# Another emission order for the same steps of a fused RWKV-6 and SwiGLU kernel, with casts, copies and masks dealt anew over the engines

## The chip, the cores and the metric

The kernel runs on one core of a Trainium2 chip. The core has five engines with a list of instructions each: TensorE (PE in the profile) for matrix products and transposes, VectorE (DVE), ScalarE (ACT), GpSimd (POOL) and SyncE (SP), which here only issues transfers. Each engine works through its own list in order and waits where an operand isn't there yet. The metric is the device time of one execution in microseconds; less is better.

## The reference

A linear-attention layer with a decaying state (RWKV-6) feeds an RMS norm and a gated feed-forward block. Cut to what is computed:

```python
batch, n_heads, seq, head_dim = (4, 8, 768, 48)
for t in range(S):
    cur = np.einsum('bhd,bhe->bhde', u[None] * kt, vt)
    y[:, :, t] = np.einsum('bhd,bhde->bhe', rt, state + cur)
    state = wt[:, :, :, None] * state + np.einsum('bhd,bhe->bhde', kt, vt)
...
n_tokens, d_model, d_ff = (3072, 384, 1536)
xn = x / np.sqrt(np.mean(x * x, axis=-1, keepdims=True) + 1e-06) * rms_g
g = xn @ w_gate
return (g * (1.0 / (1.0 + np.exp(-g))) * (xn @ w_val)) @ w_out
```

Inputs and output are float32.

## The kernel before

The sequence is cut into six blocks n of 128 positions, and there are four batches j, so there are 24 chunks (n, j) of 128 rows and 384 columns. For each chunk the kernel does the attention as matrix products over the 128 positions, then the norm; for each group of four chunks (512 rows) it does the feed-forward block.

The steps are small functions with arguments (n, j), or (n, f) in the feed-forward block, and their names are the words of the list:

- Loads on SP's queue: `load_r`, `load_k`, `load_v`, `load_w` (L256 to L280), 192 KB each; the four `load_w.0.j` bring 384 KB, two blocks at once. They go into rings of 8 buffers (4 for w). The weights of the feed-forward block come through POOL's queue: `load_gv`, `load_wo` (L348, L353).
- Decay: `ln` (ACT), `cs_mm` (PE, sums of logarithms), `cs_add` (DVE), `exp_r` and `exp_k` (ACT), `w_tot` (DVE), then `r_mul` (DVE) and `k_mul` (DVE or POOL, L457) scale r and k.
- Transposes of the scaled r and k: in blocks 0 and 1 `rk_pe` on PE and a copy `rk_tr` on DVE or ACT (L484); from block 2 on `rk_tr` is a transposing DMA from SP's queue.
- Scores and output: `q_mm` (PE; from block 2 on one step does two chunks), the mask `q_mask_e` (DVE) for the even heads, and for the odd heads either a masked copy on DVE or a plain copy on ACT (`q_copy_o`) and a mask on POOL (`q_mask_o`, L510 to L518); `cast_v` (ACT or POOL, L384); `y_mm` (PE). The bonus term is `bonus_mul` (POOL, two instructions), `bonus_sum` (DVE), `bonus_v` (POOL). The state is `st_mm` (PE) and `st_new` (DVE).
- Norm: `x_add` (DVE), `x_sq` (ACT), `x_rstd` (two instructions on ACT, or two on POOL, L560), `xn_mul` (ACT). The normed chunk is transposed into the operand of the feed-forward block by `xn_pe` and `xn_out` (PE, DVE), in blocks 4 and 5 by a transposing DMA `xn_tr` and `xn_gain` (POOL).
- Feed-forward block of group n: twelve `gate_mm` (PE, three matmuls of 512 columns), `silu` (ACT), twelve `val_mm` (PE), `h_mul` (DVE); then for each 128 rows `o_mm` (PE, twelve matmuls of 384 columns), `o_out` (DVE or ACT, L663) and `out_dma` (SP). Group 0 is made of the chunks 0.0, 0.1, 1.0, 1.1, and group 1 of 0.2, 0.3, 1.2, 1.3. The last 128 rows are done in two halves, `o_mm.5.3` and `o_mm.5.4`.

What sets the order is the list `ORDER` (L25 to L126): the kernel calls the steps in this order and every engine's list, SP's too, is that order with the other engines' steps left out. A suffix such as `:4` puts so many filler matmuls on a matrix of zeros in front of the step; they keep PE busy and compute nothing that is used. Accumulator banks come from three small rings (`psum`, L228): two banks each for gate and value products, four for everything else; the next step that needs a bank gets the one whose last reader stands earliest in the list, and PE waits for that reader. Eight sets of chunks (L175 to L189) say which engine does the steps that can be done by two: `CAST_ACT` (the cast of v on ACT rather than POOL), `K_POOL` (the k product on POOL rather than DVE), `RK_DVE` (the copy of the transposed chunk on DVE rather than ACT), `ODD_DVE` (the odd heads' mask on DVE rather than ACT and POOL), `RSTD_ACT` (the inverse root on ACT rather than POOL) and `OUT_DVE` (the output copy on DVE rather than ACT). ACT holds one table of functions at a time, one for Ln and Exp and one for Silu; `act` (L247) loads the other one (L249) when the list changes between them.

Of the kernel before, what the change touches and what calls it, by code (L numbers as in the profile page):

```python
# [41 lines left out]
gate_mm.0.2 gate_mm.0.0 rk_pe.0.2 silu.0.0 silu.0.2 val_mm.0.2 q_mask_e.0.3 h_mul.0.0 gate_mm.0.5 gate_mm.0.1 silu.0.5  # L42
silu.0.1 val_mm.0.1 rk_tr.0.2 q_copy_o.0.3 h_mul.0.1 bonus_mul.0.3 bonus_sum.0.3 h_mul.0.2 gate_mm.0.6:1
gate_mm.0.11:1 q_mm.0.2 cast_v.0.2 silu.0.6 silu.0.11 q_mask_o.0.2 gate_mm.0.8 val_mm.0.6 q_mask_e.0.2 cast_v.0.3
st_mm.0.2 val_mm.0.11 q_mask_o.0.3 h_mul.0.6 val_mm.0.5 y_mm.0.3 y_mm.0.2 bonus_sum.0.2 bonus_v.0.2 load_wo.0.0
load_wo.1.0 bonus_v.0.3 silu.0.8 h_mul.0.11 cs_mm.1.2 load_wo.2.0 h_mul.0.5 exp_k.1.2 x_add.0.2 st_new.0.2 exp_r.1.2
k_mul.1.2 cs_mm.1.3 exp_k.1.3 st_mm.0.3 exp_r.1.3 val_mm.0.8 val_mm.0.7 w_tot.1.2 r_mul.1.2 x_add.0.3 gate_mm.0.4
w_tot.1.3 r_mul.1.3 rk_pe.1.2 gate_mm.0.7 k_mul.1.3 h_mul.0.8 silu.0.4 x_sq.0.3 bonus_mul.1.2 x_rstd.0.3 rk_tr.1.2
silu.0.7 rk_pe.1.3 gate_mm.0.10 val_mm.0.4 h_mul.0.7 x_sq.0.2 rk_tr.1.3 load_k.2.1 load_k.2.3 load_v.2.1 load_v.2.0
load_k.2.2 q_mm.1.2 val_mm.0.9 cast_v.1.2 xn_mul.0.3 silu.0.10 q_copy_o.1.2 h_mul.0.4 q_mask_o.1.2 gate_mm.0.9  # L50
xn_pe.0.3 val_mm.0.10 st_new.0.3 q_mm.1.3 bonus_sum.1.2 x_rstd.0.2 q_mask_e.1.2 xn_out.0.3 y_mm.1.2 h_mul.0.10
q_mask_e.1.3 silu.0.9 h_mul.0.9 o_mm.0.3 ln.2.1 xn_mul.0.2 bonus_v.1.2 bonus_mul.1.3 q_mask_o.1.3 st_mm.1.2 xn_pe.0.2
cs_mm.2.1 ln.2.0 x_add.1.2 cs_add.2.1 x_sq.1.2 cs_mm.2.0 exp_r.2.1 o_out.0.3 xn_out.0.2 x_rstd.1.2 cast_v.1.3
cs_add.2.0 bonus_sum.1.3 w_tot.2.1 ln.2.3 exp_k.2.1 exp_r.2.0 o_mm.0.0 y_mm.1.3 xn_mul.1.2 o_out.0.0 bonus_v.1.3
r_mul.2.0 x_add.1.3 exp_k.2.0 ln.2.2 x_sq.1.3 o_mm.0.2 o_out.0.2 w_tot.2.0 r_mul.2.1 x_rstd.1.3 st_mm.1.3 cs_mm.2.3
xn_pe.1.2 cs_add.2.3 xn_out.1.2 cs_mm.2.2 exp_r.2.3 cs_add.2.2 load_k.3.3 w_tot.2.3 o_mm.0.1 xn_mul.1.3 r_mul.2.3
st_new.1.2 exp_k.2.2 val_mm.1.1 gate_mm.1.1 exp_r.2.2 exp_k.2.3 w_tot.2.2 val_mm.1.2 xn_pe.1.3 r_mul.2.2 gate_mm.1.2
st_new.1.3 silu.1.1 silu.1.2 k_mul.2.0 bonus_mul.2.0 out_dma.0.0 k_mul.2.1 cast_v.2.1 k_mul.2.3 h_mul.1.1 rk_tr.2.0
rk_tr.2.1 gate_mm.1.3 silu.1.3 bonus_mul.2.2 k_mul.2.2 xn_out.1.3 bonus_sum.2.0 h_mul.1.2 val_mm.1.5 gate_mm.1.4
silu.1.4 val_mm.1.4 rk_tr.2.3 gate_mm.1.8 st_mm.2.1 gate_mm.1.5 silu.1.8 h_mul.1.4 val_mm.1.8 load_v.2.2 silu.1.5  # L60
cast_v.2.0 st_new.2.1 rk_tr.2.2 o_out.0.1 h_mul.1.8 gate_mm.1.9 gate_mm.1.10 val_mm.1.3 load_w.3.3 load_v.2.3
load_r.3.3 load_w.3.1 out_dma.0.3 load_w.3.0 out_dma.0.1 load_r.3.0 bonus_v.2.0 bonus_mul.2.3 bonus_sum.2.2 h_mul.1.5
bonus_mul.2.1 cast_v.2.2 load_k.3.0 load_w.3.2 q_mm.2.0 load_k.3.1 silu.1.9 silu.1.10 q_copy_o.2.1 h_mul.1.3
q_mask_o.2.0 q_mask_e.2.0 q_mask_e.2.1 gate_mm.1.7 gate_mm.1.0 silu.1.0 val_mm.1.0 y_mm.2.0 gate_mm.1.6 val_mm.1.9
bonus_sum.2.3 h_mul.1.0 x_add.2.0 load_r.3.1 x_sq.2.0 silu.1.6 out_dma.0.2 h_mul.1.9 val_mm.1.10 h_mul.1.10 q_mm.2.2
gate_mm.1.11 val_mm.1.6 cast_v.2.3 q_copy_o.2.2 silu.1.7 silu.1.11 ln.3.0 x_rstd.2.0 xn_mul.2.0 q_mask_e.2.3
bonus_sum.2.1 q_mask_e.2.2 q_mask_o.2.1 load_v.3.3 load_w.4.1 load_r.3.2 ln.3.1 bonus_v.2.1 bonus_v.2.2 q_mask_o.2.3
h_mul.1.6 q_mask_o.2.2 bonus_v.2.3 st_mm.2.0 st_new.2.0 o_mm.1.0 y_mm.2.1 load_k.3.2 x_add.2.1 y_mm.2.3 val_mm.1.7
y_mm.2.2 cs_mm.3.0 st_mm.2.3 val_mm.1.11 x_add.2.3 x_sq.2.3 ln.3.3 x_sq.2.1 xn_pe.2.0 cs_mm.3.1 o_out.1.0 o_mm.1.1
out_dma.1.0 h_mul.1.7 cs_add.3.0 exp_k.3.0 x_add.2.2 cs_add.3.1 st_new.2.3 x_rstd.2.3 xn_mul.2.3 ln.3.2 x_sq.2.2  # L70
# [643 lines left out]
```

## Time and profile before

| what | value |
|---|---|
| time, median of 3 runs (lowest, highest) | 203.93 us (203.73, 204.25) |
| profiled execution: span from the first to the last instruction | 202.2 us; its time isn't listed apart |
| mean granted TensorE clock in it | 0.998 |
| DVE busy | 157.5 us, 307 instructions |
| ACT busy | 135.0 us, 278 instructions |
| POOL busy | 124.4 us, 178 instructions |
| moved by DMA | 32.42 MB, 160 GB/s over the span |

A row of the profile that groups instructions reads: line of the kernel, engine, operation, what is written from what is read by tile names, count, total busy time, mean nanoseconds of one, and then the idle time of the engine just before them with what ended it. A row of the timeline begins with start and duration in microseconds; in square brackets stand the idle time before it and its releaser. Rows of PEld are weight loads, which run beside the matmuls of PE. A row of the waits names who waited, for whom, the total, how often, and the longest. Matmuls are pipelined and their recorded ends reach past the start of the next one, so PE is read here by distances between starts.

### The profile page before, as it was taken

Reading aid. Unit: us, or ns where it says so; the run is one execution under the profiler, and the core shown is the slowest. Engines: PE = TensorE matmul, PEld = TensorE weight load, DVE = VectorE, ACT = ScalarE, POOL = GpSimd, SP = SyncE. Lnnn points to the kernel's source line nnn. Section 1 sums busy time; section 2 is a strip of 40 time slices with the busy share of each in tenths; the row PEclk is TensorE's granted clock in tenths of the full one; section 3 lists DMA queues with packets and bytes.
Section 4 is the critical chain, followed back from the end, with each engine's and each line's share of the span. In section 5 each row is a group of like instructions: output and inputs, shape, how many; then the busy total and the mean of one; then the engine's idle time right before and its main releaser. Section 6 shows DMA issues by size and latency. Waiting matters only on the chain.

```text
span 202.2 us, 4604 instructions
## 1 busy us (share of the span) xinstructions
PE 191.3 (95%) x1677; PEld 121.9 (60%) x1694; DVE 157.5 (78%) x307; ACT 135.0 (67%) x278; POOL 124.4 (62%) x178
## 2 busy tenths in 40 slices
...
GB/s 144 231 234 207 212 208 202 195 179 208 206 184 225 160 212 191 210 185 188 199 176 215 237 188 203 183 190 108 134 179 104 0 23 99 0 117 0 63 115 99
DMA packets 121567, 32.42 MB, mean 160 GB/s; under 512 B 116420, under 2 KB 120392, under 8 KB 121544
## 3 DMA queue, kind: packets, MB, share of 16 engines
...
q8 instruction: 13, 0.21, 0.4%
q14 instruction: 10, 0.08, 0.1%
...
HBM read 25.96 MB, written 4.72 MB: 152 GB/s over the span
## 4 chain that ended last, share of the span: by engine, by line
PE 65%; ACT 3%; DMA 2%; DVE 2%; issue 1%; SPq 0%; DVEq 0%; ACTq 0%
PE ps_av L617 7%; PE ps_bu L617 7%; PE ps_au L617 7%; PE ps_bv L617 6%; PE ps_qx L660 6%; PE ps_qv L660 6%; PE ps_qu L660 5%; PE ps_qz L660 4%; PE ps_au L622 2%; PE ps_bu L622 2%; DMA rkT<-rk 2%; PE ps_av L622 2%; PE ps_bv L622 2%; ACT L249 1%; PE ps_au L419 1%; PE ps_qv L500 1%
## 5 line engine op out<-in xcount | busy, mean ns | idle before, releaser
L660 PEld LDWEIGHTS <-ht 128*128 128x128 bf16 x300 | 28.1, 98 | 17.5 <-DVE ht L646 1.0
L251 ACT ACTIVATE sg<-ps_av 128x512 bf16<-128x512 f32 x36 | 21.5, 597 | 22.8 <-PE ps_av L617 18.0
L646 DVE TENSOR_TENSOR ht<-ps_bv,sg 128x512 bf16<-128x512 f32 x29 | 19.9, 687 | 13.9 <-PE ps_bv L617 12.9
L251 ACT ACTIVATE sg<-ps_au 128x512 bf16<-128x512 f32 x36 | 21.5, 596 | 11.5 <-PE ps_au L617 7.7
L617 PEld LDWEIGHTS <-wg_sb 128*128 128x128 bf16 x180 | 19.2, 114 | 15.9 <-issue 0.6
L617 PEld LDWEIGHTS <-wv_sb 128*128 128x128 bf16 x180 | 19.2, 114 | 15.7 <-issue 0.5
L465 POOL TENSOR_TENSOR ruk<-rt,kt 128x384 f32<-128x384 f32 x24 | 24.0, 1001 | 3.7 <-DMA kt<-in_k_dram 2.8
L475 POOL TENSOR_TENSOR ydiag<-vt,diag 128x384 f32<-128x384 f32 x24 | 20.4, 859 | 9.4 <-DVE diag L470 9.1
L617 PE MATMUL ps_av<-xnt,wg_sb 128*128 128x512 bf16 x88 | 25.0, 381 | 0.3
L466 POOL TENSOR_TENSOR ruk<-ruk,u_bc 128x384 f32<-128x384 f32 x24 | 24.0, 1001 | 1.9
L617 PE MATMUL ps_bu<-xnt,wv_sb 128*128 128x512 bf16 x86 | 24.8, 380 | 0.4
L646 DVE TENSOR_TENSOR ht<-ps_bu,sg 128x512 bf16<-128x512 f32 x31 | 21.3, 686 | 4.8 <-PE ps_bu L617 3.1
L617 PE MATMUL ps_au<-xnt,wg_sb 128*128 128x512 bf16 x87 | 23.6, 380 | 0.1
L617 PE MATMUL ps_bv<-xnt,wv_sb 128*128 128x512 bf16 x82 | 23.2, 380 | 0.2
L459 POOL TENSOR_TENSOR rk<-kt,ek 128x384 bf16<-128x384 f32 x16 | 15.9, 1001 | 9.7 <-ACT ek L251 5.9
L249 ACT ACT_TABLE_LOAD x14 | 18.0, 1283 | 1.9 <-PEq L698 1.6
L660 PE MATMUL ps_qx<-wo_sb,ht 128*128 128x384 bf16 x96 | 17.1, 326 | 0.2 <-DVE ht L646 0.2
L558 ACT ACTIVATE junk<-xb 128x384 bf16<-128x384 f32 x24 | 12.5, 522 | 6.3 <-DVE xb L553 6.2
L571 ACT ACTIVATE xn<-xb,rstd 128x384 bf16<-128x384 f32 x24 | 14.2, 609 | 0.6 <-POOL rstd L567 0.5
L470 DVE TENSOR_REDUCE diag<-ruk 128x8 f32<-128x384 f32 x24 | 13.1, 544 | 1.9 <-POOL ruk L466 1.9
L660 PE MATMUL ps_qv<-wo_sb,ht 128*128 128x384 bf16 (+1 forms) x84 | 13.8, 314 | 0.0
L251 ACT ACTIVATE lw<-wt 128x384 bf16<-128x384 f32 (+1 forms) x20 | 11.6, 583 | 2.8 <-DMA wt<-in_w_dram 2.7
...
## 6 DMA issues: line engine op xcount, KB each, us to landing
...
```

The lines of the kernel that those rows point to most:

```text
L249: nc.scalar.preload_act_table_set(table_name)
L251: return nc.scalar.activation(**kw).ins
L459: eng.tensor_tensor(out=rk[:, n % 2, j, 1, :, 0:D], in0=inp["k", n, j], in1=bank["cs_k", n, j][:, 0:DM].rearrange("p (h d) -> p h d", h=H) ...
L465: nc.gpsimd.tensor_tensor(out=ruk[n, j], in0=inp["r", n, j], in1=inp["k", n, j], op=ALU.mult)
L466: nc.gpsimd.tensor_tensor(out=ruk[n, j], in0=ruk[n, j], in1=u_bc, op=ALU.mult)
L470: nc.vector.tensor_reduce(out=diag[n, j].rearrange("p h o -> p (h o)"), in_=ruk[n, j], axis=mybir.AxisListType.X, op=ALU.add)
L475: nc.gpsimd.tensor_tensor(out=ydiag[n, j], in0=inp["v", n, j], in1=diag[n, j].to_broadcast([128, H, D]), op=ALU.mult)
L571: nc.scalar.activation(out=xn, in_=xb[n, j], func=AF.Copy, scale=rstd[n, j][:, 1:2])
L617: nc.tensor.matmul(ps, lhsT=units(ws, c, f), rhs=x[:, c, :], start=(c == 0), stop=(c == KC - 1))
L622: nc.tensor.matmul(ps[:, i * TS // 2:(i + 1) * TS // 2], lhsT=units(ws, c, f + i), rhs=x[:, c, cols], start=(i == 0 and c == 0), stop=(i = ...
L646: nc.vector.tensor_tensor(out=ht[n][:, f, :], in0=v, in1=sg, op=ALU.mult)
L660: nc.tensor.matmul(ps[:, cols], lhsT=ht[n][:, f, b * L:(b + 1) * L], rhs=wo_sb[:, f, cols], start=(f == 0), stop=(f == FC - 1))
```

## The change

The list has the same steps, in another order on every engine and in SP's queue; the same 50 fillers stand before the same kinds of steps, 44 of them, as before, ahead of the first feed-forward matmul. The first loads are now w before r, and v later. The changes between ACT's two function tables fall from 14 to 12. Six of the sets are dealt anew: one set entry is one chunk's step on the one or the other engine. `CAST_ACT` goes from 12 chunks to 10, `RK_DVE` from 7 to 3, `ODD_DVE` from 10 to 11, `RSTD_ACT` from 7 to 4, `OUT_DVE` from 14 to 7; `K_POOL` keeps 16, five of them other ones. The functions that do the steps are not touched. The diff, cut to the beginning of the list, the passage between the third and fourth group, the end, and the sets:

```diff
 ORDER = """
-load_r.0.0 load_w.0.0 u_mm.0.0 ln.0.0 load_v.0.0 load_k.0.0 cs_mm.0.0:2 load_r.1.0 load_w.0.1 u_out.0.0 load_k.1.0
-load_k.0.1 load_w.0.3 load_v.0.1 exp_r.0.0 exp_k.0.0 r_mul.0.0 cast_v.0.0 load_r.0.1 bonus_mul.0.0 load_k.1.1
-bonus_sum.0.0 bonus_v.0.0 k_mul.0.0 cs_mm.1.0 load_r.1.1 load_v.1.1 load_v.1.0 load_w.0.2 rk_pe.0.0:2 rk_tr.0.0
-exp_r.1.0 w_tot.1.0 w_tot.0.0 st_mm.0.0 r_mul.1.0 st_new.0.0 q_mm.0.0:4 load_k.0.3 load_r.0.3 load_r.0.2 load_k.0.2
-load_v.0.2 ln.0.1 q_mask_o.0.0 exp_k.1.0 cs_mm.0.1 exp_r.0.1 k_mul.1.0 exp_k.0.1 rk_pe.1.0 load_v.0.3 rk_tr.1.0
-bonus_mul.1.0 q_mask_e.0.0 load_k.1.3 load_r.1.2 load_k.1.2 load_r.1.3 load_v.1.2 bonus_mul.0.1 load_w.2.1 load_w.2.0
-load_v.1.3 load_w.2.3 q_mm.1.0:2 cs_mm.1.1 exp_r.1.1 exp_k.1.1 r_mul.0.1 k_mul.0.1 w_tot.0.1 q_mask_o.1.0
-bonus_sum.1.0 load_gv.0.1 cast_v.0.1 load_r.2.0 bonus_sum.0.1 r_mul.1.1 load_w.2.2 rk_pe.0.1:2 ln.0.3 y_mm.0.0
-rk_tr.0.1 st_mm.0.1:4 x_add.0.0 q_mask_e.1.0 st_new.0.1 cs_mm.0.3:3 bonus_v.0.1 cast_v.1.0 q_mm.0.1:1 y_mm.1.0
-k_mul.1.1 bonus_v.1.0 cast_v.1.1 q_copy_o.0.1 x_sq.0.0 bonus_mul.1.1 load_r.2.1 x_add.1.0 exp_r.0.3 load_r.2.2
-x_sq.1.0 load_r.2.3 load_k.2.0 q_mask_e.0.1 w_tot.1.1 rk_pe.1.1:1 rk_tr.1.1 q_mm.1.1:7 q_mask_o.1.1 load_gv.0.0
-q_mask_o.0.1 y_mm.0.1:8 g_mm.0.0 bonus_sum.1.1 ln.0.2 x_rstd.1.0 xn_mul.1.0 x_rstd.0.0 xn_mul.0.0 exp_k.0.3
-bonus_v.1.1 load_gv.1.0 q_mask_e.1.1 x_add.0.1 x_sq.0.1 x_rstd.0.1 y_mm.1.1 x_add.1.1 k_mul.0.3 xn_pe.1.0:2 xn_pe.0.0
-cs_mm.0.2 g_out.0.0 xn_out.1.0 x_sq.1.1 xn_mul.0.1 xn_out.0.0 r_mul.0.3 st_mm.1.1:3 x_rstd.1.1 st_mm.1.0 xn_mul.1.1
-xn_pe.0.1 xn_out.0.1 w_tot.0.3 rk_pe.0.3:3 xn_pe.1.1 xn_out.1.1 exp_r.0.2 exp_k.0.2 r_mul.0.2 val_mm.0.0:4 gate_mm.0.3
-silu.0.3 val_mm.0.3 rk_tr.0.3 w_tot.0.2 st_new.1.1 load_gv.1.1 k_mul.0.2 bonus_mul.0.2 q_mm.0.3 h_mul.0.3 st_new.1.0
...
-bonus_v.3.1 q_mask_o.3.1 out_dma.1.3 y_mm.3.1 val_mm.2.0 load_w.4.2 x_add.3.2 q_mask_o.3.3 silu.2.0 silu.2.6 h_mul.2.0
-ln.4.0 cast_v.4.3 val_mm.2.6 h_mul.2.6 y_mm.3.3 cs_mm.4.1 load_r.4.3 load_k.4.3 val_mm.2.5 cs_mm.4.0 x_add.3.1
-x_sq.3.1 cs_add.4.1 load_w.5.3 exp_k.4.1 x_sq.3.2 x_rstd.3.2 h_mul.2.5 bonus_mul.4.0 x_rstd.3.1 out_dma.1.1 st_mm.3.0
-load_v.4.1 xn_mul.3.1 ln.4.2 exp_r.4.1 load_w.4.3 xn_out.3.0 st_new.3.0 x_add.3.3 cs_add.4.0 bonus_mul.4.1 w_tot.4.1
...
-rk_tr.4.1 xn_mul.3.3 xn_mul.3.2 o_mm.2.1 o_mm.2.3 k_mul.4.0 xn_pe.3.1 xn_out.3.1 o_out.2.1 out_dma.2.1 cs_mm.4.2
-o_mm.2.0 r_mul.4.0 load_k.4.2 rk_tr.4.0 w_tot.4.0 bonus_sum.4.0 load_v.5.2 o_out.2.3 cs_mm.4.3 cs_add.4.2 cs_add.4.3
...
-silu.5.11 val_mm.5.11 h_mul.5.11 out_dma.4.2 val_mm.5.6 h_mul.5.6 o_mm.5.0 o_out.4.1 out_dma.4.1 out_dma.3.1 o_mm.5.4
-o_out.5.0 o_out.5.4 out_dma.5.4 out_dma.5.0 o_mm.5.1 o_out.5.1 out_dma.5.1 o_mm.5.2 o_out.5.2 out_dma.5.2 o_mm.5.3
-o_out.5.3 out_dma.5.3
+load_w.0.0 ln.0.0 load_r.1.0 load_w.0.1 load_k.1.0 load_r.0.0 u_mm.0.0 cs_mm.0.0:2 load_k.0.0 cs_mm.1.0 load_r.0.1
+g_mm.0.0 load_k.0.1 load_v.0.0 load_w.0.2 load_k.1.1 load_r.1.1 exp_r.0.0 load_v.1.0 u_out.0.0 exp_k.0.0 bonus_mul.1.0
+load_v.0.1 load_w.0.3 load_v.1.1 ln.0.1 load_r.0.3 bonus_mul.0.0 r_mul.0.0 w_tot.0.0 k_mul.0.0 exp_k.1.0 rk_pe.0.0:2
+exp_r.1.0 load_k.0.3 load_r.0.2 k_mul.1.0 r_mul.1.0 rk_tr.0.0 cs_mm.0.1 g_out.0.0 bonus_sum.0.0 w_tot.1.0
+bonus_sum.1.0 load_k.0.2 exp_r.0.1 rk_pe.1.0 bonus_mul.0.1 r_mul.0.1 q_mm.0.0:4 load_v.0.3 rk_tr.1.0 cast_v.0.0
+exp_k.0.1 q_mm.1.0:2 q_mask_o.0.0 q_mask_e.1.0 k_mul.0.1 q_mask_e.0.0 cs_mm.1.1 exp_k.1.1 exp_r.1.1 bonus_v.0.0
+k_mul.1.1 rk_pe.0.1:2 load_v.0.2 rk_tr.0.1 bonus_mul.1.1 y_mm.0.0 st_mm.0.0 r_mul.1.1 q_mask_o.1.0 st_new.0.0
+x_add.0.0 load_gv.0.1 bonus_v.1.0 cast_v.1.0 x_sq.0.0 cast_v.0.1 x_rstd.0.0 ln.0.2 ln.0.3 rk_pe.1.1:1 q_mm.0.1:1
+bonus_sum.0.1 q_mask_e.0.1 y_mm.1.0 st_mm.0.1:4 load_w.2.1 load_r.1.2 load_r.1.3 load_k.1.2 q_mask_o.0.1 w_tot.1.1
+rk_tr.1.1 y_mm.0.1:8 w_tot.0.1 cast_v.1.1 x_add.1.0 bonus_sum.1.1 bonus_v.0.1 x_sq.1.0 xn_mul.0.0 x_rstd.1.0
+q_mm.1.1:7 x_add.0.1 st_new.0.1 x_sq.0.1 q_mask_o.1.1 q_mask_e.1.1 st_mm.1.0 cs_mm.0.3:3 xn_pe.0.0 load_gv.0.0
+load_gv.1.0 bonus_v.1.1 y_mm.1.1 exp_r.0.3 cs_mm.0.2 x_rstd.0.1 st_new.1.0 exp_k.0.3 xn_mul.1.0 load_k.1.3 x_add.1.1
+load_v.1.2 load_gv.1.1 r_mul.0.3 xn_out.0.0 st_mm.1.1:3 xn_pe.1.0:2 xn_mul.0.1 x_sq.1.1 xn_pe.0.1 k_mul.0.3 x_rstd.1.1
+xn_mul.1.1 load_w.2.0 exp_r.0.2 exp_k.0.2 xn_out.0.1 xn_out.1.0 rk_pe.0.3:3 xn_pe.1.1 xn_out.1.1 w_tot.0.2 r_mul.0.2
+rk_tr.0.3 w_tot.0.3 val_mm.0.3:4 gate_mm.0.3 k_mul.0.2 bonus_mul.0.3 silu.0.3 gate_mm.0.1 q_mm.0.3 gate_mm.0.2
...
+x_add.3.2 silu.2.8 cast_v.3.3 x_rstd.3.0 q_mask_o.3.3 bonus_v.3.3 gate_mm.2.11 val_mm.2.8 gate_mm.2.0 y_mm.3.1
+st_mm.3.3 val_mm.2.0 h_mul.2.8 st_new.3.3 silu.2.11 xn_mul.3.0 silu.2.0 h_mul.2.0 val_mm.2.6 cs_mm.4.1 st_mm.3.0
+y_mm.3.3 ln.4.0 ln.4.3 xn_pe.3.0 val_mm.2.11 cs_mm.4.0 x_add.3.1 x_add.3.3 h_mul.2.6 h_mul.2.11 cs_add.4.0 cs_add.4.1
+x_sq.3.1 x_sq.3.2 x_sq.3.3 o_mm.2.3 bonus_mul.4.3 exp_r.4.0 exp_k.4.1 exp_r.4.1 o_out.2.3 ln.5.1 load_v.4.2 o_mm.2.1
+exp_k.4.0 bonus_mul.4.0 x_rstd.3.3 x_rstd.3.1 x_rstd.3.2 st_new.3.0 ln.4.2 xn_mul.3.3 xn_mul.3.2 xn_mul.3.1 load_v.4.1
+w_tot.4.0 bonus_sum.4.3 r_mul.4.0 w_tot.4.1 cast_v.4.3 k_mul.4.0 k_mul.4.1 o_out.2.1 o_mm.2.0 r_mul.4.1 xn_out.3.0
+bonus_sum.4.0 xn_pe.3.3 cs_mm.4.3 xn_out.3.3 cs_mm.4.2 xn_pe.3.1 xn_pe.3.2 cs_add.4.2 xn_out.3.1 cs_add.4.3 xn_out.3.2
+ln.5.0 o_mm.2.2 st_mm.3.1 exp_k.4.2 exp_r.4.2 exp_k.4.3 exp_r.4.3 r_mul.4.2 w_tot.4.2 r_mul.4.3 load_w.5.3 val_mm.3.5
...
+gate_mm.3.11 w_tot.4.3 out_dma.2.1 load_v.4.0 gate_mm.3.5 val_mm.3.11 silu.3.11 k_mul.4.3 st_new.3.1 load_k.5.2
+bonus_v.4.3 cast_v.4.2 k_mul.4.2 bonus_mul.4.1 silu.3.5 rk_tr.4.1 rk_tr.4.0 gate_mm.3.7 gate_mm.3.9 h_mul.3.11
+o_out.2.0 cast_v.4.0 h_mul.3.5 o_out.2.2 q_mm.4.0 silu.3.7 silu.3.9 val_mm.3.9 gate_mm.3.8 val_mm.3.7 gate_mm.3.1
...
+o_mm.5.0 o_mm.5.2 o_mm.5.1 o_out.5.0 o_out.5.2 out_dma.5.0 out_dma.5.2 o_mm.5.3 o_out.5.1 o_out.5.3 out_dma.5.1
+out_dma.5.3 o_mm.5.4 o_out.5.4 out_dma.5.4
 """
...
-    CAST_ACT = sel("00 01 02 03 20 21 30 31 33 40 43 53")
+    CAST_ACT = sel("00 01 10 11 20 23 30 31 32 41")
-    K_POOL = sel("02 10 20 21 22 23 30 31 32 33 40 42 43 50 51 53")
+    K_POOL = sel("02 03 11 12 20 21 22 23 31 32 33 40 41 42 50 52")
-    RK_DVE = sel("00 02 03 10 11 12 13")
-    ODD_DVE = sel("00 02 10 11 13 20 23 40 43 52")
-    RSTD_ACT = sel("00 10 11 13 20 32 33")
-    OUT_DVE = sel("00 01 10 13 20 21 22 30 33 40 42 50 52 53")
+    RK_DVE = sel("02 03 11")
+    ODD_DVE = sel("00 01 03 10 11 12 13 20 40 41 43")
+    RSTD_ACT = sel("00 03 10 11")
+    OUT_DVE = sel("00 12 21 31 32 41 43")
```

More of the change, by code (lines that the diff above doesn't have):

```diff
@@ L41 @@
-silu.0.3 val_mm.0.3 rk_tr.0.3 w_tot.0.2 st_new.1.1 load_gv.1.1 k_mul.0.2 bonus_mul.0.2 q_mm.0.3 h_mul.0.3 st_new.1.0
[L42 to L70, printed above, removed]
@@ new lines @@
+exp_r.1.2 y_mm.0.2 st_mm.0.3 val_mm.0.6 ln.2.1 load_wo.2.0 gate_mm.0.8 r_mul.1.2 w_tot.1.2 gate_mm.0.6 x_add.0.2
+st_new.0.3 st_new.0.2 k_mul.1.3 silu.0.8 rk_pe.1.2 silu.0.6 h_mul.0.6 x_add.0.3 h_mul.0.8 gate_mm.0.9 gate_mm.0.10
+rk_pe.1.3 val_mm.0.5 bonus_mul.1.2 rk_tr.1.2 silu.0.9 rk_tr.1.3 x_sq.0.2 h_mul.0.5 cs_mm.2.1 q_mm.1.2 silu.0.10
+val_mm.0.10 q_mm.1.3 val_mm.0.9 x_sq.0.3 q_mask_e.1.2 q_mask_o.1.2 bonus_sum.1.2 ln.2.0 h_mul.0.10 h_mul.0.9
+x_rstd.0.2 bonus_mul.1.3 bonus_v.1.2 q_mask_e.1.3 load_r.2.2 bonus_sum.1.3 y_mm.1.2 cs_add.2.1 o_mm.0.3 x_add.1.2
@@ new lines @@
+cs_mm.2.0 x_rstd.0.3 o_out.0.3 xn_mul.0.3 xn_mul.0.2 o_mm.0.0 x_sq.1.2 cs_add.2.0 q_mask_o.1.3 load_k.2.0 load_v.2.1
+xn_pe.0.3 xn_pe.0.2 out_dma.0.3 cast_v.1.3 x_rstd.1.2 bonus_v.1.3 exp_r.2.0 o_out.0.0 exp_r.2.1 xn_out.0.2 xn_out.0.3
+w_tot.2.1 w_tot.2.0 r_mul.2.0 r_mul.2.1 o_mm.0.2 xn_mul.1.2 ln.2.3 exp_k.2.0 ln.2.2 exp_k.2.1 y_mm.1.3 x_add.1.3
+cs_mm.2.3 cs_add.2.3 xn_pe.1.2 cs_mm.2.2 o_out.0.2 o_mm.0.1 x_sq.1.3 bonus_mul.2.1 xn_out.1.2 cs_add.2.2 exp_k.2.3
+k_mul.2.1 exp_r.2.3 exp_r.2.2 exp_k.2.2 x_rstd.1.3 r_mul.2.3 w_tot.2.3 w_tot.2.2 r_mul.2.2 st_mm.1.3 val_mm.1.0
```

112 lines of the change are left out of this document (64 added, 48 removed).

## The prediction

> **What bounds the kernel now.** I read the page's busy times first, then what PE waited for, then the chain of work that ended last and the timeline at its joints.
>
> ```profile
> PE 191.3 (95%) x1677; PEld 121.9 (60%) x1694; DVE 157.5 (78%) x307; ACT 135.0 (67%) x278; POOL 124.4 (62%) x178
> ```
>
> ```profile
> PE ps_qu L372 <- POOL ones_row L338: 4.2, 1, 4.2
> PE ps_qz L500 <- DVE rkT L489: 0.9, 1, 0.9
> PE ps_qu L500 <- DMA rkT<-rk: 0.6, 1, 0.6
> PE ps_qx L500 <- DVE rkT L489: 0.5, 1, 0.5
> PE ps_qx L548 <- POOL vb L389: 0.3, 1, 0.3
> PE ps_qv L548 <- POOL qts L518: 0.2, 1, 0.2
> PE ps_qx L660 <- DVE ht L646: 0.2, 1, 0.2
> ```
>
> ```profile
> 92.85 0.65 PE ps_au L617 x3
> ...
> 194.11 1.95 PE ps_qx L660 x12
> ```
>
> ```profile
> 22.64 0.23 PE L500 MATMUL ps_qz<-rkT 48*128 48x128 bf16 x1 [0.85 <-DVE rkT L489]
> 30.21 0.81 PE L617 MATMUL ps_bv<-xnt,wv_sb 128*128 128x512 bf16 x2
> 123.84 0.23 PE L500 MATMUL ps_qu<-rkT 48*128 48x128 bf16 x1 [0.59 <-DMA rkT<-rk]
> 197.84 1.15 PE L660 MATMUL ps_qu<-wo_sb,ht 128*128 128x192 bf16 x12
> 199.03 0.36 DVE L667 COPY ob<-ps_qu 128x192 f32<-128x192 f32 x1 [0.38 <-PE ps_qu L660]
> ```
>
> PE is the bound, in two different ways. It starts at 4.2 after a memset on POOL; up to 30.21, its first feed-forward matmul, it does the attention of four chunks and 44 fillers, and it waits: 0.9 + 0.5 + 0.3 + 0.2 = 1.9 us in this list. From 30.21 to the last matmul (198.99 = 197.84 + 1.15) it waits 0.6 + 0.2 = 0.8 us in 168.8; a gate or value step of three matmuls takes 0.65 and an output step of twelve 1.95, one behind the other. After it come one copy and one store.
>
> The PE steps and fillers ahead of the first feed-forward matmul are the same in both lists (29 steps, 44 fillers), and so are those behind it. A new order therefore cannot shorten PE's own work in either part: it can only remove waits, or make some. That frames the sum: at most about 1.9 + 0.8 us to win among the waits listed, and no such limit on what can be lost.
>
> A rule that speaks against this reading is in the Trainium skill, "Perfetto Trace Analysis", section Identifying the Most-Contended Engine: matmul busy time is no measure of how near PE is to its limit, and weight-load busy time is a better one, which here would be 60%. By it PE would have room and the gain would not end at the waits. It is the last rival below.
>
> **The dealing.** The rows that price an edit:
>
> ```profile
> L491 ACT COPY rkT<-ps_qv 128x1024 bf16<-128x1024 bf16 x1 | 1.0, 1013 | 0.0
> L489 DVE COPY rkT<-ps_qv 128x1024 bf16<-128x1024 bf16 x3 | 2.1, 689 | 0.7 <-PE ps_qv L482 0.7
> L387 ACT CAST vb<-vt 128x384 bf16<-128x384 f32 x12 | 6.1, 507 | 0.0
> L389 POOL CAST vb<-vt 128x384 bf16<-128x384 f32 x12 | 6.0, 503 | 4.4 <-DMA vt<-in_v_dram 4.4
> L515 DVE TENSOR_TENSOR qts<-ps_qu,mask_lt 128x512 bf16<-128x512 f32 x5 | 3.4, 680 | 0.0
> L511 ACT CAST qts<-ps_qu 128x512 bf16<-128x512 f32 x4 | 2.4, 590 | 0.0
> L518 POOL TENSOR_SCALAR_AFFINE_SELECT qts<-qts 128x512 bf16<-128x512 bf16 x14 | 8.8, 638 | 4.4 <-ACT qts L511 4.3
> L251 ACT ACTIVATE rstd<-rstd,eps_col 128x1 f32<-128x1 f32 x7 | 2.0, 284 | 0.0
> L251 ACT ACTIVATE rstd<-rstd 128x1 f32<-128x1 f32 x7 | 1.4, 203 | 0.2
> L566 POOL TENSOR_SCALAR rstd<-rstd 128x1 f32<-128x1 f32 x17 | 3.2, 191 | 9.8 <-ACT junk L558 9.2
> L567 POOL TENSOR_TENSOR rstd<-rstd,mhalf 128x1 f32<-128x1 f32 x17 | 9.6, 563 | 1.4
> L667 DVE COPY ob<-ps_qv 128x384 f32<-128x384 f32 x4 | 2.2, 554 | 1.7 <-DMA out_dram<-ob 1.6 <-PE ps_qv L660 0.2
> L669 ACT COPY ob<-ps_qx 128x384 f32<-128x384 f32 x4 | 1.9, 476 | 1.6 <-PE ps_qx L660 1.6
> L249 ACT ACT_TABLE_LOAD x14 | 18.0, 1283 | 1.9 <-PEq L698 1.6
> ```
>
> ACT loses two table loads (2.57), two casts (1.01), one odd-head copy (0.59) and three roots (3 x 0.487 = 1.46), and takes four transposed copies (4.05) and seven output copies, one of them a half (some 3.2): +1.6, to 136.6 us. DVE gives up four transposed copies (2.76) and the output copies (6 x 0.554 + 0.36 = 3.68) and takes one mask (0.68): -5.8, to 151.8. POOL gets two casts (1.01) and three roots (3 x 0.754 = 2.26) and loses one mask (0.64): +2.6, to 127.0. The k products are sixteen on POOL as before. All three stay far below the span, beside PE's work, so by themselves these moves cost nothing; what hides them is PE's list, and where PE waits they show. They enter the sum only there.
>
> **The front.** Four waits of others for loads give the pace of the load queue:
>
> ```profile
> 5.42 0.84 ACT L251 ACTIVATE lw<-wt 128x768 bf16<-128x768 f32 x1 [2.50 <-DMA wt<-in_w_dram]
> 7.08 1.00 POOL L465 TENSOR_TENSOR ruk<-rt,kt 128x384 f32<-128x384 f32 x1 [2.84 <-DMA kt<-in_k_dram]
> 9.61 0.84 ACT L251 ACTIVATE lw<-wt 128x768 bf16<-128x768 f32 x1 [0.21 <-DMA wt<-in_w_dram]
> 9.66 0.54 DVE L459 TENSOR_TENSOR rk<-kt,ps_bu 128x384 bf16<-128x384 f32 x1
> 14.61 1.00 POOL L465 TENSOR_TENSOR ruk<-rt,kt 128x384 f32<-128x384 f32 x1 [0.68 <-DMA rt<-in_r_dram]
> ```
>
> With 192 KB = 0.197 MB a load (0.393 for these w), the four came at 0.59, 0.98, 1.57 and 2.75 MB: a straight line of 4.25 us per MB. On it load_k.0.0, sixth in the new list at 1.57 MB, comes at 9.6, and its k_mul starts where it does now (9.66), so chunk 0.0 loses nothing by coming behind three loads. load_v.0.0 comes at 12.1, and its first reader, bonus_v.0.0, stands behind three bonus_mul on POOL, about 14.3. The price of the later v is nothing while POOL is busy there; if it weren't, it would be up to 5.9 us of bonus_v.0.0 (12.1 against 6.2 now, third at 0.79 MB), with x_add.0.0 next in line.
>
> I then followed the new front by hand with the durations above, load arrivals from the line, and banks by the ring's rule. Gone: the 0.9 (rk_tr.1.1 stands earlier on DVE and is done near 20.5, while PE comes for it behind y_mm.0.1 and its eight fillers, near 22.5); the 0.5 (rk_tr.1.0, now on ACT, is done at 13.4, and PE comes at 13.5); the 0.3 and 0.2 (cast and mask are done before PE gets there). New: rk_pe.0.1 waits about 0.6, since q_mask_o.0.0, q_mask_e.1.0 and k_mul.0.1 (0.68 + 0.68 + 0.54) now stand in a row on DVE; y_mm.0.0 waits 0.3 for q_mask_e.0.0 behind them; and the bank of st_mm.0.1 is held by q_mask_e.0.1 for about 0.3. Sum 1.2. Net 1.9 - 1.2 = -0.7: first feed-forward matmul near 29.5. The bounds are -1.9 (no new wait) and +0.8 (the new waits at 2.7, if each is 0.5 longer: a hand walk misses small delays). I take -0.7, the walk's own value.
>
> **From the first feed-forward matmul on.** The 0.59 at 123.84 is q_mm.4.0 waiting for the transposes of block 4. In the new list PE has, between cs_mm.4.0 and this step, four output steps and six gate or value steps (4 x 1.95 + 6 x 0.65 = 11.7) where it had four and four (10.4): 1.3 more cover, so the wait should go. On SP rk_tr.4.1 now stands behind out_dma.2.1, whose copy is on DVE ahead of this, and behind two loads whose buffers were read a group before. The next in line there is the third root on POOL, below. The load queue issues its loads for block 4 in one stretch early in group 2 instead of between output stores. Against the 0.8 gone I set 0.5 of new waits: the bounds are 0 and, by the longest listed wait of such a kind now, 0.9 at two places, 1.8. So -0.3 (-0.8 to +1.0).
>
> The two table loads that go stood in a chain here:
>
> ```profile
> 130.15 1.28 ACT L249
> 131.44 0.94 ACT lw L251 x2
> ...
> 132.90 1.28 ACT L249
> ```
>
> ACT goes straight from a load into work, 0.01 us later. "ScalarE: Activation LUTs", What ACT_TABLE_LOAD costs, in the Trainium skill, adds a drain of about 1.38 us to each switch, some 2.66 in all; this trace shows no such gap. By the page ACT's load would fall by 1.2 (1.6 - 2 x 1.38), by the rows it rises by 1.6.
>
> **The end.** The last step is again a half output step with its copy and a 96 KB store. The copy moves to ACT: 0.32 for 0.36 by the neighbouring full ones (476 against 554). I take -0.05, bounds -0.3 (less queued ahead of the last store) and 0.
>
> **The sum.** 202.2 - 0.7 - 0.3 - 0.05 = 201.2 us of span. The median of the timed runs lies 1.7 above this span (203.93 - 202.2), and I keep that: 202.9 us.
>
> **The rivals.**
>
> *Waits for waits.* PE's work is the same, and each wait that goes is paid elsewhere: 203.9. For it: the new list has three new waits even in my walk. Against it: the largest ones listed have clear causes that the list moves.
>
> *POOL becomes late between groups 2 and 3: slower.* Behind y_mm.3.3 the new list puts on POOL two bonus_mul (4 x 1.0), then x_rstd.3.3, 3.1 and 3.2, two of which were on ACT, then a cast and two k products. xn_pe.3.1 needs the roots, and PE has 3 output steps and small ones ahead of it, about 7.9 us. By the rows x_sq.3.3 is ready some 2.8 behind y_mm.3.3, three roots take 3 x 0.754, some 3 with the gaps between instructions, and the three xn_mul on ACT end at about 7.0: 0.9 of slack, all an estimate by hand. If POOL comes late to the first root by more than that, PE waits by the excess, and o_mm.2.2 and all of group 3 behind it. POOL can be that late:
>
> ```profile
> POOL rk L459 <- DMA kt<-in_k_dram: 3.8, 1, 3.8
> ```
>
> With such a wait PE loses 2.9 and the time is 205.8; with 3 us, 205.0. It decides the sign from 1.9 us (0.9 slack and 1.0 of gain). Against it: the loads for block 4 stand earlier in the new queue.
>
> *Every wait of the front goes and none comes later:* -1.9 - 0.8 - 0.3: 200.9; half-way, 201.9.
>
> *PE isn't the bound.* If DVE set the pace, its 5.8 us less would show: 198.1. The rows speak against it: PE's steps stand back to back for 168.8 us with 0.8 of waits.
>
> **How the numbers follow.** 0.3% of 203.93 is 0.6 us, about what a measurement of this kernel can tell from no change: faster is below 203.3, slower above 204.5. Forecast 202.9 (202.2 to 203.6): 0.50, of which 0.07 lies above 203.3. Waits for waits: 0.22, with 0.03 on each side. Late POOL: 0.18. The larger gain: 0.08. DVE: 0.02. Faster: 0.43 + 0.03 + 0.08 + 0.02 = 0.56; same: 0.07 + 0.16 = 0.23; slower: 0.18 + 0.03 = 0.21. The range reaches from the half-way case, 201.8, to the late POOL with 3 us, 205.0. The forecast's own range stands above.
>
> **What would show it.** Right: first feed-forward matmul between 29.0 and 30.0; no wait for rkT from DVE of 0.9 among PE's waits; no PE wait for the transposes of block 4; PE's waits behind the first feed-forward matmul below 0.8; twelve table loads; DVE near 152, ACT near 137, POOL near 127. Wrong: a first feed-forward matmul at 30.2 or later, or PE waits at xn_pe.3.1 (on ACT's xn, and behind it POOL's roots) of 2 us, or a new wait for a load anywhere on PE's path.

## The result and the profile after

The changed kernel takes 202.49 us (median of 8 executions, 201.46 to 203.69) against 204.19 us for the kernel before beside it (8 executions, 203.70 to 204.85). The ratio is 0.9921, 95% interval 0.9892 to 0.9950: faster, with the whole interval below 1, and 0.4 us below the forecast of 202.9. A second timing, in the first experiment below, gave 204.72 us against 204.88, a ratio of 0.999 (0.996 to 1.002), which is no difference. Both belong to the result. Ratios leave out executions over 1.5% longer than the quickest of the same kernel; medians hold all of them, so a ratio need not be the quotient of two medians.

The profiled execution took 202.01 us, 200.3 of it span: 1.7 outside the span, as before. The page of the changed kernel begins with the engines' busy times, and its chain and its table loads read so:

```profile
PE 190.3 (95%) x1678; PEld 122.5 (61%) x1694; DVE 152.9 (76%) x297; ACT 136.8 (68%) x278; POOL 127.1 (63%) x185
...
PE 92%; POOL 1%; DMA 1%; DVE 1%; issue 1%; ACT 0%; POOLq 0%; ACTq 0%
...
L249 ACT ACT_TABLE_LOAD x12 | 15.4, 1283 | 1.8 <-PEq L698 1.6
```

PE was 65% of the chain that ended last; now it is 92%. ACT and POOL moved as worked out (136.6 and 127.0 forecast), DVE by 4.6 instead of 5.8, and no engine but PE is near the span.

What PE of the changed kernel waited for (in total, times, longest):

```profile
PE ps_qu L372 <- POOL ones_row L338: 4.2, 1, 4.2
PE ps_qz L240 <- DVE qts L507: 0.5, 1, 0.5
PE ps_qx L238 <- ACT rkT L491: 0.5, 1, 0.5
PE ps_qz L500 <- DMA rkT<-rk: 0.3, 1, 0.3
PE ps_bu L617 <- issue: 0.2, 1, 0.2
```

The four front waits of before are gone. Two others have come, both for a bank that a filler (L238, L240) wants first. A third, of y_mm.0.0 for the mask q_mask_e.0.0, stands only in the row of its weight load:

```profile
16.42 0.27 PEld L548 LDWEIGHTS <-qts 128*128 128x128 bf16 x8 [0.28 <-DVE qts L507]
```

Behind the first feed-forward matmul only the 0.3 is left of 0.8. The 0.2 with "issue" is no wait: it stands at 38.74, where the step shows two of its three matmuls, so a record is missing, and from step to step nothing is lost there.

The joints on the timeline of the changed kernel (start, length, instruction, wait ahead of it):

```profile
29.73 0.81 PE L617 MATMUL ps_bu<-xnt,wv_sb 128*128 128x512 bf16 x2
...
123.51 0.23 PE L500 MATMUL ps_qz<-rkT 48*128 48x128 bf16 x1 [0.27 <-DMA rkT<-rk]
...
195.67 1.15 PE L660 MATMUL ps_qv<-wo_sb,ht 128*128 128x192 bf16 x12
...
196.90 0.32 ACT L669 COPY ob<-ps_qv 128x192 f32<-128x192 f32 x1 [0.67 <-PE ps_qv L660]
```

So the span's gain of 1.9 has three parts. The first feed-forward matmul starts at 29.73 instead of 30.21: -0.48. From there to the last matmul's end (196.82 = 195.67 + 1.15) it is 167.09 instead of 168.78: -1.69. What comes behind is 3.48 instead of 3.25: +0.23.

Where the 1.69 lay can be read in the kernel before, as steps that took longer than their like. Two places of its timeline:

```profile
52.68 1.62 PE L660 MATMUL ps_qx<-wo_sb,ht 128*128 128x384 bf16 x9
...
54.48 0.66 PE L660 MATMUL ps_qx<-wo_sb,ht 128*128 128x384 bf16 x3 [0.17 <-DVE ht L646]
...
133.96 0.81 PE L617 MATMUL ps_bu<-xnt,wv_sb 128*128 128x512 bf16 x3
...
134.20 0.60 ACT L251 ACTIVATE sg<-ps_au 128x512 bf16<-128x512 f32 x1
...
134.84 0.81 PE L617 MATMUL ps_au<-xnt,wg_sb 128*128 128x512 bf16 x3
```

The output step of twelve at 52.68 takes 0.34 more than the usual 1.95, half of it shown as a wait for ht. At 133.96 a step that takes 0.65 elsewhere takes 0.88: PE needs the bank ps_au, and the silu that empties it comes only at 134.20, behind the two table loads at 130.15 and 132.90 that the prediction quotes. The list of waits doesn't show this one. With 0.33 less at q_mm.4.0 (step to step 0.75 over the usual before, 0.42 now) and a bank wait of 0.19 at 41.3, four places hold 1.09 of the 1.69; the rest is in pieces of at most 0.15.

### The profile page after: what moved, and what is told of

Its sections match the earlier page's. It is cut to its first block, busy times and chain, and to the rows that moved or that the text cites. A ratio compares the mean times of both kernels' runs of the same rounds, so it can differ in the third digit from the quotient of the medians.

```text
span 200.3 us, 4599 instructions
## 1 busy us (share of the span) xinstructions
PE 190.3 (95%) x1678; PEld 122.5 (61%) x1694; DVE 152.9 (76%) x297; ACT 136.8 (68%) x278; POOL 127.1 (63%) x185
## 4 chain that ended last, share of the span: by engine, by line
PE 92%; POOL 1%; DMA 1%; DVE 1%; issue 1%; ACT 0%; POOLq 0%; ACTq 0%
PE ps_bu L617 10%; PE ps_au L617 10%; PE ps_bv L617 9%; PE ps_av L617 9%; PE ps_qx L660 9%; PE ps_qv L660 5%; PE ps_qu L660 5%; PE ps_qz L660 4%; PE ps_au L622 2%; PE ps_bu L622 2%; PE ps_bv L622 2%; PE ps_av L622 2%; DMA rkT<-rk 1%; PE ps_qx L500 1%; PE ps_qv L548 1%
## 5 line engine op out<-in xcount | busy, mean ns | idle before, releaser
L251 ACT ACTIVATE sg<-ps_au 128x512 bf16<-128x512 f32 x39 | 23.3, 596 | 13.8 <-PE ps_au L617 10.3
L617 PEld LDWEIGHTS <-wg_sb 128*128 128x128 bf16 x180 | 19.7, 114 | 16.6 <-issue 0.3
L251 ACT ACTIVATE sg<-ps_av 128x512 bf16<-128x512 f32 x33 | 19.7, 598 | 14.7 <-PE ps_av L617 12.0
L475 POOL TENSOR_TENSOR ydiag<-vt,diag 128x384 f32<-128x384 f32 x24 | 19.9, 833 | 11.8 <-DVE diag L470 7.2
L617 PE MATMUL ps_au<-xnt,wg_sb 128*128 128x512 bf16 x93 | 25.8, 379 | 0.2
L617 PE MATMUL ps_av<-xnt,wg_sb 128*128 128x512 bf16 x82 | 22.7, 380 | 0.1
L660 PE MATMUL ps_qx<-wo_sb,ht 128*128 128x384 bf16 x108 | 19.0, 326 | 0.0
L566 POOL TENSOR_SCALAR rstd<-rstd 128x1 f32<-128x1 f32 x20 | 3.8, 191 | 13.8 <-ACT junk L558 12.7
## 6 DMA issues: line engine op xcount, KB each, us to landing
wg_sb<-in_moe_w_gate_dram POOLq DMA_DIRECT2D x1, 768.0 KB, 10.8
```

What stands on the lines that cost most here:

```text
L251: return nc.scalar.activation(**kw).ins
L475: nc.gpsimd.tensor_tensor(out=ydiag[n, j], in0=inp["v", n, j], in1=diag[n, j].to_broadcast([128, H, D]), op=ALU.mult)
L617: nc.tensor.matmul(ps, lhsT=units(ws, c, f), rhs=x[:, c, :], start=(c == 0), stop=(c == KC - 1))
L660: nc.tensor.matmul(ps[:, cols], lhsT=ht[n][:, f, b * L:(b + 1) * L], rhs=wo_sb[:, f, cols], start=(f == 0), stop=(f == FC - 1))
```

## The experiments

All ratios are to the kernel before, run beside each; the rows were timed in three groups of four, and the changed kernel itself stands only in the last. "Order" is the list of steps, "dealing" the six sets that say which engine does a cast, product, copy, mask or root. Where a chunk's odd mask changes between DVE and ACT with POOL, its copy step is put in right ahead of the mask, or the mask takes the copy's place.

| kernel | median us | before, us | ratio (95%) |
|---|---|---|---|
| new order, old dealing | 215.25 | 205.70 | 1.0467 (1.0396 to 1.0537) |
| old order, new dealing | 222.36 | 205.70 | 1.0824 (1.0765 to 1.0883) |
| new front, old rest | 207.11 | 205.70 | 1.0009 (0.9963 to 1.0055) |
| old front, new rest | 206.99 | 205.70 | 1.0050 (1.0005 to 1.0095) |
| changed, old k products | 208.96 | 205.50 | 1.0161 (1.0082 to 1.0239) |
| changed, old casts and roots | 209.28 | 205.50 | 1.0159 (1.0065 to 1.0253) |
| changed, old copies and masks | 206.59 | 205.50 | 1.0058 (1.0014 to 1.0102) |
| changed, old output copies | 206.25 | 205.50 | 1.0030 (0.9980 to 1.0081) |
| changed again | 204.72 | 204.88 | 0.9990 (0.9960 to 1.0020) |
| changed, spare loads | 215.54 | 204.88 | 1.0510 (1.0455 to 1.0565) |
| before, spare loads | 214.35 | 204.88 | 1.0484 (1.0432 to 1.0537) |
| changed, transposes earlier | 203.69 | 204.88 | 0.9931 (0.9902 to 0.9961) |

### The changed kernel again

No edit. Expected:

> The changed kernel once more, beside the three that follow. If its gain is a property of the list, the ratio to the kernel before is 0.989 to 0.995 here too, and its waits are the same ones (0.5 at the bank of rk_pe.1.1, 0.5 at that of st_mm.0.1, 0.3 to 0.4 for the transposes of block 4). Rival: it stands or falls with when the loads land, and comes out anywhere from 0.985 to 1.005.

Measured 0.999 (0.996 to 1.002): the rival. The three waits named are there, the one for the transposes over four times as long, and one for output weights is new. PE's waits in this profile (span 203.3), that for the first memset left out:

```profile
PE ps_qz L500 <- DMA rkT<-rk: 1.2, 1, 1.2
PE ps_qz L240 <- DVE qts L507: 0.5, 1, 0.5
PE ps_qx L238 <- ACT rkT L491: 0.5, 1, 0.5
PE ps_qz L660 <- DMA wo_sb<-in_moe_w_out_dram: 0.2, 1, 0.2
```

Against the first profile of the same kernel, 3.0 us shorter: the first feed-forward matmul is 0.93 later (30.66), the step ahead of q_mm.4.0 takes 0.96 more, and the output step at 52.77, which now waits for its weights, 0.4 more; the rest is in small pieces. Where the 0.93 comes from is in the last section. For the 0.96, SP's rows of the two profiles, first profile first:

```profile
118.93 2.95 SPq L487 DMA_TRANSPOSE rkT<-rk  x2
```

```profile
121.11 3.75 SPq L487 DMA_TRANSPOSE rkT<-rk  x2
```

The two transposes go out 2.2 later, with PE 2.05 later at that group (its first matmul at 121.25 against 119.20), and take 0.8 longer to issue. What made PE late is passed on, and the issue adds its own; why it took longer wasn't followed.

### Order and dealing apart

```
...
-    CAST_ACT = sel("00 01 10 11 20 23 30 31 32 41")
+    CAST_ACT = sel("00 01 02 03 20 21 30 31 33 40 43 53")
...
-    OUT_DVE = sel("00 12 21 31 32 41 43")
+    OUT_DVE = sel("00 01 10 13 20 21 22 30 33 40 42 50 52 53")
```

That is the new order with the six old sets; the other kernel has the old order with the six new ones. Expected of the two:

> The changed kernel's list of steps with the dealing (casts, k products, transposed copies, odd masks, roots, output copies) of the kernel before. Theory (the order makes the gain: it takes the small waits out of PE's list, about 1.7 us behind the first feed-forward matmul and 0.5 before it; the dealing only moves work that lies beside PE): 202.2 to 203.2 us, PE's busy share near 95%, first feed-forward matmul 29.5 to 30.2. Rival 1 (DVE's 5 us less make the gain): 203.9 or more, with PE waits on DVE as before. Rival 2 (the order fits only the dealing that it was chosen with): above 204.5.

> The list of the kernel before with the changed kernel's dealing. Theory (the order makes the gain): 203.6 to 204.8 us, DVE's busy time near 152 and no gain from it; the waits for the transposes of block 4 and for ht stay. Rival 1 (the dealing makes the gain): 202.2 to 203. Rival 2 (each fits only its own): above 205.

Measured: both slower than the kernel before, by 4.7% and 8.2%. The theory that the order alone makes the gain falls, the dealing alone makes none, and the last rival holds: each fits only its own. What the mixtures lose where wasn't followed step by step; ACT loads its function tables 14 times in the first and 16 in the second, and PE falls to half rate (last section) once in the first and twice in the second.

### One set of the dealing at a time

```
-    K_POOL = sel("02 03 11 12 20 21 22 23 31 32 33 40 41 42 50 52")
+    K_POOL = sel("02 10 20 21 22 23 30 31 32 33 40 42 43 50 51 53")
```

and likewise for the casts with the roots, the transposed copies with the odd masks, and the output copies, each in the new order. Expected:

> The changed kernel, with the k products alone dealt as before (five from DVE to POOL, five from POOL to DVE: 10, 30, 43, 51, 53 and 03, 11, 12, 41, 52). The prediction's view (a step that is dealt elsewhere lies beside PE's work and costs nothing by itself): ratio to the kernel before 0.990 to 0.995, as the changed kernel. Theory since then (the list holds each step back to just where its engine is free, so a step twice as long in a place chosen for the short one is late for PE): over 1.00, that is a loss of 2 us or more against the changed kernel, since a k product is 1.12 us on one engine and 0.54 on the other.

> The changed kernel, with the casts of v and the roots alone dealt as before (five casts from ACT to POOL, seven from POOL to ACT; roots of 13, 20, 32, 33 back on ACT, 03 on POOL). The prediction's view (cost nothing by themselves; the late POOL between groups 2 and 3 would even be eased): ratio 0.988 to 0.995. Theory since then: the casts are early enough to be free, but roots on ACT stand behind gates of the feed-forward part and bring table switches; a loss of 0.5 to 3 us, ratio 0.995 to 1.007.

> The changed kernel, with the transposed copies of 00, 10, 12, 13 back on DVE and the odd masks dealt as before (01, 03, 12, 41 by ACT and POOL, 02, 23, 52 on DVE). The prediction's view: within 0.6 us of the changed kernel, ratio 0.989 to 0.995. Theory since then: these stand between two PE steps of a chunk, and a mask in two parts (0.59 on ACT, then 0.64 on POOL) is later by more than the 0.68 on DVE, so PE waits for masks and for banks: a loss of 2 to 6 us, ratio 1.00 to 1.02.

> The changed kernel, with the output copies alone dealt as before (seven of them back on DVE). The prediction's view: within 0.6 us of the changed kernel. Theory since then: a copy placed on DVE in a list made for ACT lies ahead of products that PE needs, 0.55 late each, and holds a bank of PE; a loss of 1 to 3 us, ratio 0.997 to 1.007.

Measured: every one loses against the changed kernel, by 2.4, 2.4, 1.4 and 1.1% if its first ratio (0.9921) is taken, by 1.7, 1.7, 0.7 and 0.4% by the second (0.999); only the output copies' 0.4% is within the uncertainty. The four sum to 7.3 or 4.5%, the six sets at once to 5.5 or 4.8%: about the same sum by the second ratio, less by the first. Some of the new waits of PE, from the timelines of the four kernels, in that order:

```profile
12.83 0.40 PE L482 MATMUL ps_qz<-ident,rk 128*128 128x128 bf16 x4 [0.94 <-POOL rk L459]
...
129.73 0.23 PE L500 MATMUL ps_qz<-rkT 48*128 48x128 bf16 x1 [1.66 <-DMA rkT<-rk]
```

```profile
21.28 0.48 PE L548 MATMUL ps_qv<-vb,qts 128*128 128x48 bf16 x8 [2.50 <-POOL vb L389]
```

```profile
22.07 2.45 PE L240 MATMUL ps_qu<-zero 128*128 128x384 bf16 x8 [1.38 <-ACT qts L511]
```

```profile
154.32 0.21 PE L502 MATMUL ps_qu<-rkT 48*128 48x128 bf16 x1 [0.89 <-DVE ob L667]
```

A k product on POOL instead of DVE holds up rk_pe by 0.94, and the transposes of block 4 come 1.66 late (a k product takes 1.00 on POOL; the 1.12 of the expectation is in no row); casts back on POOL hold up y_mm by 2.50, where I had expected the casts to be free and the roots to cost; a mask by ACT and POOL keeps a filler's bank for 1.38; a copy on DVE keeps a bank of q_mm for 0.89. The waits are not the whole loss. In the second and third kernel PE runs at half rate behind the wait shown: the eight fillers at 22.07 take 2.45, in the changed kernel 1.46. The second also has 14 table loads on ACT again instead of 12.

### The front and the rest apart

One kernel takes the steps up to its first feed-forward matmul in the changed kernel's order and dealing and all others as before; the other the reverse. Expected:

> The changed kernel's list up to the first feed-forward matmul, then every step that is left in the order of the kernel before; each step dealt as in the kernel whose list it stands in. Theory (most of the gain lies behind the first feed-forward matmul): first feed-forward matmul near 29.7, and the time 203.4 to 204.0, 0.5 below the kernel before. Rival (what the front does with loads and buffers decides what comes later): 202.2 to 202.9, the whole gain with the old rest.

> The list of the kernel before up to the first feed-forward matmul, then every step that is left in the changed kernel's order. Theory: first feed-forward matmul near 30.2, and the time 202.4 to 203.2, the gain of the steady part without that of the front. Rival (the front decides): 203.6 or more, with new waits at the joint.

Measured: 1.0009 (0.9963 to 1.0055) and 1.0050 (1.0005 to 1.0095). Neither half brings its part of the gain. The first is too uncertain to tell 0.5 us from nothing, and its joint is at fault too: six of its twelve executions took 208.23 to 211.29 us at granted clocks of 0.984 to 0.992, the others 204.42 to 205.99 at 0.997 or more, and in the profiled one (211.16) PE waits 5.42 until 38.85 for a k product on POOL, which had waited 10.67 for its load. The second is slower than before, with new waits at the joint, so the rest of the list is fitted to its own front too. How the gain splits between them can't be had this way.

### Later loads

```
+    def load_x(n, j):
+        t = pin.tile([128, H, D], FP32, name="spare", bufs=1)
+        nc.sync.dma_start(out=t, in_=k[j, :, n * L:(n + 1) * L, :].rearrange("h t d -> t h d"))
...
+xn_out.2.3 r_mul.3.1 o_out.1.0 exp_k.3.1 xn_mul.2.2 xn_mul.2.1 load_x.4.0 load_x.4.1 load_w.4.1 load_v.3.2
```

and so for blocks 2 and 3, in both kernels. Expected:

> The changed kernel with six more loads of 192 KB that nothing reads, two ahead of the first load of each of blocks 2, 3 and 4, so that all behind them come later: by 6 x 0.197 MB x 4.25 us per MB = 5.0 us if the queue never has a pause. Theory A (a list that was chosen under late loads bears them better): it loses at most 2 us against the changed kernel, and less than half of what the kernel before loses by the same. Theory B (both live from the same slack in the load queue): both lose the same within 1 us.

> The kernel before with the same six loads, two ahead of its first load of each of blocks 2, 3 and 4. Theory A: a loss of 3 to 6 us, more than twice that of the changed kernel. Theory B: a loss within 1 us of the changed kernel's.

Measured: the changed kernel loses 10.8 us (215.54 - 204.72), the kernel before 9.5 (214.35 - 204.88). Theory A falls: the new list bears late loads no better. Both lose more than the 5.0 worked out, since the two spare loads of a pair share a buffer and the second waits for the first, with the queue behind it. From the changed kernel's timeline, SP's row for the pair of block 4 and, later, three steps on PE:

```profile
90.75 5.37 SPq L278 DMA_DIRECT2D spare<-in_k_dram  x2
...
103.43 1.44 PE L621 MATMUL ps_au<-xnt,wg_sb 128*128 128x512 bf16 x3 [3.52 <-ACT sg L251]
104.67 1.49 PE L621 MATMUL ps_av<-xnt,wg_sb 128*128 128x512 bf16 x3
...
106.90 0.81 PE L621 MATMUL ps_au<-xnt,wg_sb 128*128 128x512 bf16 x3
```

The pair holds SP for 5.4 us; other pairs of loads hold it for 1.2 to 1.9 in the changed kernel. PE then waits 3.52, and the next two steps of three matmuls take 1.44 and 1.49 instead of 0.81.

### The transposes of block 4 earlier

```
-gate_mm.3.11 w_tot.4.3 out_dma.2.1 load_v.4.0 gate_mm.3.5 val_mm.3.11 silu.3.11 k_mul.4.3 st_new.3.1 load_k.5.2
-bonus_v.4.3 cast_v.4.2 k_mul.4.2 bonus_mul.4.1 silu.3.5 rk_tr.4.1 rk_tr.4.0 gate_mm.3.7 gate_mm.3.9 h_mul.3.11
+gate_mm.3.11 w_tot.4.3 out_dma.2.1 rk_tr.4.1 rk_tr.4.0 load_v.4.0 gate_mm.3.5 val_mm.3.11 silu.3.11 k_mul.4.3
+st_new.3.1 load_k.5.2 bonus_v.4.3 cast_v.4.2 k_mul.4.2 bonus_mul.4.1 silu.3.5 gate_mm.3.7 gate_mm.3.9 h_mul.3.11
```

Expected:

> The changed kernel with two steps moved: the transposes of 4.1 and 4.0 stand in SP's queue ahead of the loads of v 4.0 and k 5.2 instead of behind them, 1.1 us earlier by the trace (0.43 + 0.68). Theory (the wait of 0.4 at q_mm.4.0 is what SP holds ahead of the transposes): the wait goes and the time falls by 0.2 to 0.4, ratio lower than the changed kernel's by 0.001 to 0.002, the trace showing no PE wait for rkT of block 4. Rival (they wait for POOL's k products, not for SP): the wait stays at 0.3 to 0.4, and the two loads behind are 3 us later, for a loss of 0 to 1.

Measured: 0.9931 (0.9902 to 0.9961), beside 0.999 for the changed kernel in the same place: 0.6% less, more than expected. The wait it removes was 1.2 there. PE's waits in its profile, those for the first memset and for the two fillers' banks left out:

```profile
PE ps_qz L660 <- DMA wo_sb<-in_moe_w_out_dram: 0.8, 1, 0.8
...
PE ps_qv L586 <- ACT xn L571: 0.3, 1, 0.3
PE ps_qz L482 <- DVE rk L453: 0.3, 1, 0.3
```

There is none for rkT of block 4. The queue's order on SP was the cause of that wait. By its times this version beats both kernels. Its one profile doesn't show where: of the 2.0 us by which its span of 201.3 lies below the 203.3 of the changed kernel run beside it, 1.61 lies ahead of the first feed-forward matmul (29.05 against 30.66), where nothing was moved, and the steady part is 0.36 shorter (168.81 against 169.17), with 0.6 more of waiting for output weights.

## Why the prediction was right, and where it was wrong

The sign, the time and the frame (PE's own work unchanged, only waits to win) came out, in the first timing. That the time did is partly luck: the span changed by -1.94 where the terms sum to -1.05, the steady part made up the difference, and the second timing, 204.72, lies outside the range. Point by point:

*The front.* -0.48 against -0.7. The four old waits went as walked, the bank of st_mm.0.1 was foreseen (0.5 for 0.3), and so was y_mm.0.0 (0.28 for 0.3). rk_pe.0.1 did not wait. The bank of rk_pe.1.1's filler did, for the copy of 0.1 on ACT: 0.47 at a place that I had not listed. So the new waits sum to the 1.2 of the walk, with one of the three at another place. Besides, PE came to its full rate about 1.0 later in this execution than in the profile before (last section), worth about 0.5; without that the front's gain would be near 1.0. In the second profile full rate came 3.2 later than before and the first feed-forward matmul 0.45 later, which by the same working is again a gain of about 1.0. Both are estimates from single executions. (The fillers ahead of that matmul are 48, not 44, in both lists, with the four of its own step.)

*The steady part* is the term that was mis-sized: -0.3, measured -1.69. The step that failed is the bound "1.9 + 0.8 us to win among the waits listed". The list of waits held 0.8 there, but by the timeline steps ran over their usual time by about 3.5 us, of which 1.8 is left in the changed kernel's first profile: bank waits such as the one at 134.84, and pieces of 0.1 to 0.3, aren't in the list. The 0.5 set aside for new waits didn't come in that execution. In the second profile the steady part is 169.17 (199.83 - 30.66), 0.39 longer than before, with 1.2 at q_mm.4.0. So -1.69 is what one execution had, not a property of the list, and two executions can't tell what the list is worth there.

*"The wait should go"* at q_mm.4.0 was wrong. It shrank to 0.27 in one profile and grew to 1.2 in the other. I gave PE 1.3 more cover, named the two loads that now stand ahead of the transposes on SP, and put the time that SP holds for them (0.43 + 0.68) at nothing; the experiment that moves the transposes ahead removes the wait.

*The dealing* "by themselves these moves cost nothing" was wrong as a statement of its own. Single old sets in the new order bring it to 0.3 to 1.6% over the kernel before, the six new sets in the old order to 8.2%. Here each dealing was free only in the order made for it. The sums for ACT and POOL held within 0.2 us, that for DVE was 1.2 too large, and there were twelve table loads.

*The end* was +0.23 against -0.05. The copy is shorter as worked out (0.32 for 0.36), but what follows it is longer, 3.4 to 3.5 from the last matmul's end in three profiles of this order against 3.25. The cause wasn't followed.

*The rivals.* Waits for waits, 203.9, is what the second timing shows: the time of before, with its largest wait at the transposes. Late POOL did not cost anything in the first profile, by little. The changed kernel's rows on POOL, ACT and PE:

```profile
110.21 1.00 POOL L465 TENSOR_TENSOR ruk<-rt,kt 128x384 f32<-128x384 f32 x1 [0.80 <-DMA rt<-in_r_dram]
```

```profile
114.57 1.62 ACT L571 ACTIVATE xn<-xb,rstd 128x384 bf16<-128x384 f32 x3
```

```profile
116.75 0.33 PE L586 MATMUL ps_qv<-ident,xn 128*128 128x128 bf16 x3
```

POOL did wait for a load, 0.80; the third xn was ready at 116.19, and xn_pe.3.1 came at 116.75: 0.56 left of a slack that I had put at 0.9. In the second profile POOL waited 1.73 for that load, the third xn was ready at 118.74 and xn_pe.3.1 came at 118.79: the slack was gone. With the transposes earlier, the same place waits 0.3. So this rival is near, and hangs on when a load lands. That PE isn't the bound has no support: DVE fell by 4.6 and the time by 1.7 or by nothing, while the mixtures with waits on PE of 0.9 to 2.5 were 0.3 to 1.6% slower than the kernel before, the least of them within its uncertainty.

What stays open: how much of the difference between the two timings is the order, and how much when loads land in that session. Two profiles of one kernel differ by 3.0 us of span, which is more than the effect.
